# Last batch's attention output in tiles of 128 queries, transposed by DMA, in a fused attention and long-convolution kernel

## The chip, the cores and the metric

One core of one Trainium2 chip runs the whole kernel. Its engines run side by side, each through its own list of instructions in order, and wait for each other by semaphores: TensorE (PE: matmuls and transposes, into eight banks of PSUM), VectorE (DVE), ScalarE (ACT), GpSimd (POOL, here the queue that issues loads) and SyncE (SP, here the queue of stores and of DMA transposes). The metric is device time in microseconds (us) of one execution, the median of several runs.

## The reference, cut to what matters

Banded attention with eight global keys, and on its output a gated long convolution by FFT over the 768 positions. Shapes: batch 4, 8 heads, 768 positions, 64 per head (512 in all).

```python
# attention: keys 0..7 are seen by all, beyond them the last 96 positions
keep = (pos_k < 8) | ((rel >= 0) & (rel < 96))
scores = where(keep, q @ k.T / 8 - slope[h] * dist, -1e9)
a = softmax(scores); x = (a @ v)            # -> [B, 768, 512]
# gated long convolution
x1, x2, x3 = split(x @ w_proj, 3)
conv = irfft(rfft(x2, axis=1) * rfft(filter, axis=0), n=768)
out = (x1 * conv * x3) @ w_out              # [4, 768, 512] float32
```

## The kernel before

All four batches go through one pipeline; the work of batch b+1's attention is mixed with that of batch b's convolution.

**The order.** The program first collects operations in a `Plan` (each a small function with an engine or a choice of engines, the keys that it reads and writes, and the banks that it takes). `schedule` (L155) then replays a text, `ORDER` (L41): each word is an operation's number, an engine's letter (P, A, V, G for POOL, S for SP) and the PSUM banks; `i2b7` are two dummy matmuls into bank 7, which fill time at the start. So every engine's sequence, and the engine that does an operation that could go to ACT or DVE (`"AV"`), stands in this text.

**Attention.** Keys lie in seven tiles of 120 (the eight global keys stand beside each), `KL` = 120. For head pair `hp` and group `gi`, `scores` (L740) multiplies K by Q with the keys on the partitions: a tile of keys against the 216 queries that can see it (168 and 48 for the last two, `EW`). ACT takes the exponential (L773) into the tile `E`, DVE multiplies by a mask (L785, for two head pairs at once in batches 1 to 3). In `E` the queries of tile m start at column 248 m: 216 of data and a gap of 32 that is zero (set by `gaps`, L470 to L482; four operations, one for each head pair, each a memset of the gaps, L480, and one of ones at the end, L481).

`values` (L793) takes `E` as the stationary operand: 120 queries against the keys of their own tile (L808) and of the tile before (L813), 65 columns each, the 65th being the row sum. Queries come in the groups `GRP` = tiles (0,1), (2,3), (4,5,6); j is a half of the heads. Then a reciprocal on DVE (L837) and the scaling into `xn` on DVE (L832, one instruction) or ACT (L836, an instruction for every tile and head). `transpose_x` (L842) turns the tiles on PE (L854) into one bank and copies that (helper `copy`, L313) to `xT`, which has the 512 features on partitions and the 768 positions as columns. For batch 3 K and Q are not turned on PE but by 13 `dma_start_transpose` on SP's queue (`cross`, L395, L405).

**Convolution.** Gates x1, x3 are matmuls of `xT` with `w_proj` (`gate`, L922, L932), for a half s of the positions; x2 goes through a `butterfly` on DVE (L861 to L888) and a projection (`proj`, L993), then forward spectra (L1125), products with the filter's spectrum, inverse transforms (L1023, L1030), `mixed` (L1076, DVE, among it a doubling, L1092), `gated` (L1097, y = conv x gates), and the output matmuls (L1059). Their bank is scaled into an output tile `ot` of 128 positions by ACT (L317) or DVE (L319), and SP stores it (L1071). There are six buffers `ot`, taken in turn; the last tile of the last batch goes in two halves, in one buffer. `neg` is the negation of two inverse tables, which batch 3 uses.

Of the kernel before, what the change touches and what calls it, by code (L numbers as in the profile page):

```python
# [17 lines left out]
P = 128  # L18
# [10 lines left out]
def act(n):  # L29
    return 0.06 + n / 1200.0  # L30
# [11 lines left out]
0V 1V 2A 45S 3G 5V 4V 30V i2b7 17P0 18A 7G 47S 32G 49S 12P1 22P2 33A 56S 37V 34V 8V 19V 10V 20V 51G 21A 55G  # L42
46V 41V 53G 6V 40V 42V 23A 35G 24V 48V 13A 83P0 84A 25V i3b7 81P3 54G 14A 38A 36V 82V 52G 15V i2b7 149P23 85P1
27A 39V 44V 50V 115P45 57V 72G 58V 16A 26A 150A 60G 61G 93P0 87P6 86V 63G 89P7 88V 9V 95P1 80A 97P23 62G 31A
116A 43V 90V 91P6 92V 64G 98A 96V 74A 65G 151P45 152A 117P23 118A 99P67 101P45 119P23 94V 100A 102A 103P01 66G
11V 238G 155P45 67G 59S 120A 78A 28V 239G 211V 121P23 237G 29V 236G 104A 110P01 69G 235G 156A 212V 68G 105P67
213V 111V 122A 79A 234G 76A 153P45 128P23 106V 112V 123P01 107V 201P6 129V 233G 214V 232G 124V 108P7 130V 154A
215V 131P2 113P3 70G 125V 109A 244G 75A 157P45 114A 245G 126P7 132A 248G 127A 216V 158V 162P01 206A 246G 208A
133P7 73A 247G 135A 217V 240G 339P2 241G 243G 242G 137P3 159V 340A 220P7 229P45 163V 160P2 139A 164V 337P3
230A 202A 71G 252G 161V 251G 338V 226P01 221A 218P4 165P7 231V 145P3 203A 207A 219A 141P2 227A 166V 147A  # L50
371P45 184V 192V 134P3 254G 204A 335P0 193V 143A 457G 333P2 228A 249S 183V 195V 194V 209A 138P1 253G 334V 185V
336A 171P7 222P0 186V 140V 205A 136V 372A 223A 142P6 351P23 196V 369P01 173A 187V 144V 405P45 188V 197V 146P7
175P6 453G 198V 189V 352A 200V 345P2 148V 190V 347P3 370A 406A 177A 407P01 349P45 172P7 341P6 408A 350A 167P0
346V 77A 342A 168P1 452G 348V 250S 409V 169V 356P45 376P23 191V 256G 357A 451G 255G 174V 450G 343P0 344V 224P6
170V 377A 179P7 225A 455G 181A 374P45 354P23 456G 410P01 454G 353V 375A 199V 258P6 355A 259A 270P7 373V 359P45
378V 274P2 271A 411A 360V 412P67 413A 260P3 463G 284P0 361V 379P67 358V 414V 384P45 275A 469G 385V 380V 285A
282P2 261A 262P0 283A 364P23 386V 381V 460G 263A 470G 365V 278P4 264P5 552P6 466G 286V 279A 366V 462G 265A
467S 287V 459G 362P7 420P01 550P2 266P3 421V 464G 422V 363A 458G 415P45 553A 180P6 367P7 416V 556P0 267A 272P3
554P1 551A 368A 461G 268V 176P7 417V 557A 566P45 387P0 269V 273A 182V 276P3 555A 178V 418P1 388V 465G 382P2
568P67 567A 277A 588P45 419V 586P01 423P3 667G 474G 383V 389P2 569A 681G 587A 300P6 473G 471G 391A 280V 390P7  # L60
424V 393P2 296P3 671G 281V 672G 622P01 468S 589A 472G 624P45 673G 682G 570V 301A 394P6 392V 395A 292P7 302P2
297A 441V 625A 623A 442V 396V 558P3 293A 675G 562P4 563A 303A 294P5 290P0 425P1 291A 427A 288P6 295A 298P7
560P4 289A 443V 559V 689G 426P3 429P2 626V 444V 668G 576P01 561A 397P6 428V 431A 564P4 445V 299A 690G 577V
565A 687G 399A 475P2 446V 398P3 573P45 476A 593P67 578V 447V 574A 677G 304V 674G 688G 449V 571P01 448V 685G
401P2 400V 572A 430P4 594A 305V 479P5 432V 591P01 629P67 403A 306V 590V 627P23 480A 402P4 670S 487P5 680G 676G
592A 630A 579P0 477P1 575V 628A 488A 478A 307V 596P23 669S 595V 597V 483P5 404V 684S 581P67 580A 257G 308V
678G 489P1 437P4 582V 686G 598A 433P0 309V 490A 484A 679G 583V 601P23 435A 499P6 310V 584P5 602V 491P7 434P0
631V 500A 438P6 585V 603A 501P5 599P1 311V 637P23 436V 313V 439A 492A 502A 769S 481P7 600A 604P0 632P45 493P1
766S 768S 605A 773S 482A 312V 778S 618P0 638V 633V 494A 503V 639V 440V 634A 485V 611P7 614P1 504V 767S 610P2
771S 612A 495P6 318P3 770S 496A 606P2 486V 640P6 513P4 635P5 620A 619P0 319A 497V 616A 775S 776S 613V 514A  # L70
641A 636A 772S 315P1 608A 784P67 498V 781P45 621V 316A 658V 782A 779P23 785A 654P0 656A 615P1 509P4 507P5
505P6 607P7 314V 617V 517P0 780A 510A 659V 655P1 609V 661V 508A 657V 515P7 650P5 506A 516A 519P4 511P1 660V
518A 520V 662V 652A 663V 512A 774S 799P67 801P23 521V 800A 802A 642P5 664V 330P4 777S 841P67 683S 644A 786P23
522V 324P1 331A 665V 651P0 839P45 666V 842A 783V 325A 846P67 787A 703P1 840A 847A 704A 327P2 646P3 844P67 328A
806P45 523V 807A 653V 804P01 524V 695P2 691P4 693P5 317S 843V 805A 332S 525V 648A 789P01 788V 803V 808V 790V
705P3 845A 848V 692A 321P4 694A 696A 794P67 699P2 526V 795V 527V 791A 707P5 700A 796V 706A 849P01 322A 708A
530V 697P6 850V 814P23 647P7 698A 815V 809P45 851V 810V 531V 643P6 816A 854P01 544P2 645V 797P6 811A 792P3
649V 547P7 717P4 709P5 855V 798A 323S 329S 326S 793A 715P3 528V 711P6 856V 545A 710A 529V 817P2 852P0 712A
701V 812P5 716A 718A 541P1 857P3 320S 818A 532P4 713V 813A 719V 858A 542A 548A 720V 535P5 853A 825P3 714V 546S
834P2 533A 702V 879V 880V 829P0 725P4 727P1 882V 735P7 836A 726A 733P2 827A 881V 883V 721P6 538P4 536A 731P5  # L80
884V 210A 722A 732A 885V 835P3 729P6 539A 736A 728A 734A 870P5 730A 723P4 724A 888P7 887V 886V 830P2 738V
899P4 737V 739V 901P6 889A 910P7 900A 534S 543S 892P4 902A 740V 832A 905P6 837A 890P1 893A 741V 912P4 911A
913A 537S 819P3 549S 896P7 838V 865P4 891A 872A 897A 540S 894P1 903P5 895A 864P7 742V 821A 820P1 743V 904A
914V 907P5 867A 906A 908A 824P4 744V 898V 915V 831A 916P6 869P5 920P0 931P3 935P2 746V 909V 826A 745V 921A
937P4 917A 747V 932A 859P0 828V 933P3 922P6 938A 918P4 936A 833V 757P2 934A 940V 923A 751P6 860P3 939V 919A
925V 822A 748P1 754P4 924V 941V 752A 926V 942V 758A 760P2 755A 874P4 823V 943V 753S 927V 928V 944V 929V 862A
749A 945V 750S 756S 930V 948V 871A 763P3 759S 946V 876A 949V 947V 761A 762S 866A 875P1 961V 868V 877A 861A
764A 959V 863V 873V 950P2 951A 953P1 765S 954A 956P3 878V 952S 960V 975P2 955S 967P0 957A 962V 958S 976P 968P
971P3 963P1 972P 977A 969V 978S 970S 964P 973V 965A 974S 966S
# [108 lines left out]
class Fused:  # L198
# [16 lines left out]
    GRP = [(0, 1), (2, 3), (4, 5, 6)]  # L215
    Q0 = [0, 240, 480]
# [20 lines left out]
    def buffers(self):  # L237
# [48 lines left out]
        self.ot = [t(f"ot{i}", [P, DM], F32) for i in range(6)]  # L286
# [142 lines left out]
    def setup(self):  # L429
# [40 lines left out]
        for i in range(4):  # L470
            et = self.E[i]

            def gaps(e, et=et):
                if e == "A":
                    self.fill(et[:, :, 0:1488].rearrange("p h (m w) -> p h m w", m=6)[:, :, :, 216:248], 0.0)
                    self.fill(et[:, :, 1456:1536], 1.0)
                    return
                et = et.bitcast(F32)
                gap = et[:, :, 0:744].rearrange("p h (m w) -> p h m w", m=6)[:, :, :, 108:124]
                v.memset(gap, 0.0)  # L480
                v.memset(et[:, :, 728:768], ONES)  # L481
            g.op("AV", {"A": act(384) + act(160), "V": 0.38}, gaps, r=["idle"], w=[("E", i, c) for c in range(3)], name="gaps", bias=-3300)  # L482
# [59 lines left out]
    def inverse_tables(self):  # L542
# [31 lines left out]
        g.op("AV", {"A": 4 * act(P), "V": 4 * dve(P, 4)}, scaled, r=["part"], w=[("fwd", 3), "foldp"], name="foldp")  # L574
        g.op("AV", {"A": 2 * act(P), "V": dve(2 * P, 4)}, lambda e: [self.times(
            e, self.neg[:, n], self.inv[:, 2 - 2 * n], -1.0) for n in range(2)] if e == "A" else self.times(
            e, self.neg[:, ::-1], self.inv[:, 0:4:2], -1.0), r=[("inv", i) for i in range(7)], w=["neg"], name="neg")

    def distances(self):


# [279 lines left out]
    def butterfly(self, js):  # L861
# [4 lines left out]
        def op(cost, fn, r, w):  # L866
            g.op("V", cost, fn, r=[(k, j) for k in r for j in js], w=[(w, j) for j in js], name="bfly")
# [429 lines left out]
```

## Time and profile before

| | us |
|---|---|
| median of 3 runs | 166.29 (166.76, 165.31, 166.29) |
| the profiled execution | 164.31 |
| its span in the profile | 162.5 |
| PE busy | 154.4 (95%), 1608 matmuls |
| DVE busy | 151.9 (93%), 332 instructions |
| ACT busy | 149.8 (92%), 332 instructions |
| POOL busy | 77.2 (47%), 101 instructions |

The profiler records one execution: the span from the first to the last event, and in it the busy time of each engine. A row of the grouped views begins with the source line and the engine; L808 is line 808 of the kernel. Where a helper issues an instruction (L313 `copy`, L317 and L319 `times`, L328 `fill`), the tiles' names tell which step it is. In a row `out<-in 128x512 f16<-128x512 f32 x11 | 7.3, 675 | 0.0` stand the tiles, their partitions by elements, the count, the busy us, the mean ns and the idle time before them. The times of matmuls overlap, since PE works on several at once; how fast a stream of them goes is seen from their starts. A bracket in a row of the timeline is the engine's idle time just before it and what ended it; a link of the chain of waits has its start, its length and what it is.

### The profile page before, as it was taken

How to read it: one execution, taken by the hardware profiler on the slowest of the kernel's cores; microseconds unless marked ns; L12 is line 12 of the kernel's file. 1: busy time of each engine (PE TensorE's matmuls, PEld its weight loads, DVE VectorE, ACT ScalarE, POOL GpSimd, SP SyncE). 2: the span in 40 equal slices, each digit the busy share in tenths (PEclk: the TensorE clock that was granted, in tenths of full speed). 3: DMA queues.
4: the chain of work that ended last, by engine and by line, in shares of the span. 5: the costliest groups of instructions: out<-in, count | busy, mean ns of one | idle time of the engine just before them, and what ended most of it. 6: DMA issues, size and time to landing. Idle time of an engine off the chain costs nothing.

```text
span 162.5 us, 4271 instructions
## 1 busy us (share of the span) xinstructions
PE 154.4 (95%) x1608; PEld 93.4 (57%) x1608; DVE 151.9 (93%) x332; ACT 149.8 (92%) x332; POOL 77.2 (47%) x101
## 2 busy tenths in 40 slices
PE   7888989999999999999999999999999999999990
PEld 2444367565656866865657567455766664584450
DVE  5899979799999999999999999999999999999961
ACT  6979999999999999999899999999999998985961
POOL 7999198999999999999930000000000000000000
PEclk9999999999999999999999999999999999999999
DMA  5999999999999999999999984210083350001395
GB/s 164 215 148 164 167 158 171 171 166 160 184 155 149 125 139 131 143 145 139 149 150 165 141 161 93 67 44 0 11 205 115 130 196 0 4 0 61 142 363 210
DMA packets 85036, 21.95 MB, mean 135 GB/s; under 512 B 75664, under 2 KB 82072, under 8 KB 85016
## 3 DMA queue, kind: packets, MB, share of 16 engines
q0 software_dynamic: 73040, 12.11, 97.8%
q1 hardware_dynamic: 11976, 9.57, 23.0%
q8 instruction: 12, 0.20, 0.5%
q14 instruction: 8, 0.07, 0.1%
HBM read 25.40 MB, written 6.29 MB: 195 GB/s over the span
## 4 chain that ended last, share of the span: by engine, by line
PE 63%; ACT 17%; DVE 12%; issue 4%; POOL 1%; POOLq 0%
PE bank L932 18%; PE bank L1059 13%; PE bank L993 10%; ACT E L773 4%; PE bank L758 4%; PE bank L808 3%; PE bank L1125 3%; PE bank L813 3%; PE bank L854 2%; PE bank L1023 2%; PE bank L706 2%; ACT mask L626 2%; DVE E L785 2%; ACT h L317 1%; DVE g L946 1%
## 5 line engine op out<-in xcount | busy, mean ns | idle before, releaser
L932 PE MATMUL bank<-xT,w 128*128 128x384 f16 x256 | 49.5, 326 | 0.2
L773 ACT ACTIVATE E<-bank 128x864 f16<-128x864 f32 x48 | 41.4, 941 | 0.1
L932 PEld LDWEIGHTS <-w 128*128 128x128 f16 x256 | 23.3, 98 | 16.1 <-issue 1.7
L338 POOL DMA_DIRECT2D vn<-in_v_dram x28 | 27.8, 1019 | 0.4 <-DMA w<-in_moe_w_proj_dram 0.4
L338 POOL DMA_DIRECT2D kn<-in_k_dram x25 | 22.8, 930 | 3.3 <-DMA g<-in_moe_filter_fft_dram 3.3
L1059 PE MATMUL bank<-wo,y 128*128 128x512 f16 (+1 forms) x100 | 23.2, 371 | 0.0
L338 POOL DMA_DIRECT2D qn<-in_q_dram x25 | 22.4, 907 | 0.7 <-issue 0.6
L785 DVE TENSOR_TENSOR E<-E,mask 128x1728 f16<-128x1728 f16 x18 | 18.4, 1044 | 0.0
L317 ACT ACTIVATE ot<-bank 128x512 f32<-128x512 f32 (+1 forms) x23 | 14.3, 647 | 4.0 <-PE bank L1059 3.1
L317 ACT ACTIVATE x<-bank 128x384 f16<-128x384 f32 x31 | 17.0, 556 | 0.0
L993 PE MATMUL bank<-w,xs 128*128 128x512 f16 x64 | 16.5, 379 | 0.0
L313 ACT CAST ab<-bank 128x512 f16<-128x512 f32 x24 | 14.9, 648 | 1.3 <-PE bank L993 1.3
L808 PE MATMUL bank<-vn,E 128*128 128x65 f16 x224 | 15.4, 193 | 0.5 <-ACT E L773 0.5
L808 PEld LDWEIGHTS <-E 128*128 128x128 f16 x224 | 14.3, 97 | 2.5 <-issue 0.7
L313 ACT CAST eo<-bank 128x384 f16<-128x384 f32 x31 | 14.3, 555 | 1.0 <-PE bank L1030 1.0
L813 PE MATMUL bank<-vn,E 128*128 128x65 f16 x192 | 15.2, 193 | 0.0
L313 ACT CAST X<-bank 128x512 f16<-128x512 f32 x24 | 14.5, 635 | 0.1
L1059 PEld LDWEIGHTS <-y 128*128 128x128 f16 x100 | 9.2, 98 | 9.1 <-DVE y L1114 0.6
L758 PE MATMUL bank<-QT,KT 64*128 64x216 f16 (+2 forms) x224 | 14.1, 242 | 0.0
L832 DVE TENSOR_TENSOR xn<-bank,rc 128x512 f16<-128x512 f32 (+1 forms) x18 | 13.9, 779 | 0.1
L813 PEld LDWEIGHTS <-E 128*128 128x128 f16 x192 | 13.2, 97 | 0.8
L758 PEld LDWEIGHTS <-KT 64*128 64x128 f16 x224 | 7.9, 94 | 9.1 <-issue 7.6
(160 smaller groups left out, 337.1 us busy)
## 6 DMA issues: line engine op xcount, KB each, us to landing
out_dram<-ot SPq DMA_DIRECT2D x18, 256.0 KB
vn<-in_v_dram POOLq DMA_DIRECT2D x28, 120.0 KB, 5.9
kn<-in_k_dram POOLq DMA_DIRECT2D x16, 96.0 KB, 5.4
qn<-in_q_dram POOLq DMA_DIRECT2D x16, 96.0 KB, 5.1
out_dram<-ot SPq DMA_DIRECT2D x12, 128.0 KB
w<-in_moe_w_proj_dram POOLq DMA_DIRECT2D x4, 256.0 KB, 6.3
kn<-in_k_dram POOLq DMA_DIRECT2D x7, 120.0 KB, 5.4
g<-in_moe_filter_fft_dram POOLq DMA_DIRECT2D x1, 768.0 KB, 10.2
```

Of the source, the lines that this page charges most:

```text
L313: {"A": nc.scalar.copy, "V": nc.vector.tensor_copy, "G": nc.gpsimd.tensor_copy}[e](out, in_)
L317: self.nc.scalar.mul(out, in_, c)
L338: return self.g.op(eng, 0.57 + 0.00035 * nbytes[0] if eng == "G" else 0.5, lambda _: e.dma_start(dst, src), w=w, r=r, nbytes=nbytes, name= ...
L758: nc.tensor.matmul(bs[hh].f32()[:, off:off + w], self.KT[hs, hp, P * m:P * m + P], self.QT[hs, hp, KL * m:KL * m + w], start=(off == 0 and ...
L773: g.op("A", act(864), lambda _: nc.scalar.activation(eo, bs[0].two()[:, :, 0:432].rearrange("p h (m w) -> p h m w", m=2), Act.Exp, scale=s ...
L785: g.op("V", dve(1728, 2), lambda _: nc.vector.tensor_mul(ep, ep, mk), r=[("mask", h) for h in range(hs.start, hs.stop)], w=[("E", hp - 1, ...
L808: nc.tensor.matmul(o[:, n, hh], ef[:, at:at + P], vt[:, t, 2 * hp + hh, 0:D + 1], start=first, stop=(t == 0), skip_group_check=True)
L813: nc.tensor.matmul(o[:, n, hh], ef[:, at:at + P], vt[:, t - 1, 2 * hp + hh, 0:D + 1], start=False, stop=True, skip_group_check=True)
L832: nc.vector.tensor_mul(to, o[:, :, :, 0:D], rc.to_broadcast([P, 2, 2 * nt, D]))
L932: nc.tensor.matmul(bk.f32()[:, 0:h], self.w[:, c, o + P * j:o + P * j + P], self.xT[:, c, h * s:h * s + h], start=(c == 0), stop=(c == 3))
L993: nc.tensor.matmul(bk.f32(), src[:, c], w[:, c, DM:2 * DM], start=(c == 0), stop=(c == 3))
L1059: nc.tensor.matmul(bk.f32()[:, 0:n], y[:, c, P * t:P * t + P], self.wo[:, c, cs], start=(c == 0), stop=(c == 3))
```

## The change

Batch 3 only (`XCROSS`): its output goes in six tiles of 128 queries, not seven of 120, and to `xT` by DMA transposes.

- `E` has wide gaps of zeros: the starts are `EP`, 0, 336, 664, ... for all batches, so that 128 queries that start anywhere can be read from a key tile's columns, with zeros where that tile is not seen. `E` grows from 1536 to 1976 columns a head. `gaps` are eight operations, not four, with one memset for each gap. The 48 columns of the last key tile are copied behind the end (`e6`, two operations).
- `values_x` sums for each of the six tiles the key tiles that it can see, and scales into `xc`, [128 queries, 6 tiles, 512]; `xc` lies over `xn`.
- `cross_x` issues one `dma_start_transpose` for each tile (128x512, f16) on SP. The 28 PE transposes of batch 3 and its six copies to `xT` are gone. The second half's gates depend on the last group alone.
- Output buffers: three `ot` for batches 0 and 1; for batches 2 and 3 five that lie in `vn[0]`, the values of even batches, which nothing reads once batch 2's are summed. The halves of the last tile wait for the store that left their buffer.
- `neg` lies over a part of `fwd` and is computed once the filter's spectra are done. For batches 2 and 3 the butterfly's halving and the mix's doubling may go to ACT (`late`). `ORDER` is new throughout: engines, banks and places of all operations, POOL's loads among them.

```diff
-0V 1V 2A 45S 3G 5V 4V 30V i2b7 17P0 18A 7G 47S 32G 49S 12P1 22P2 33A 56S 37V 34V 8V 19V 10V 20V 51G 21A 55G
...
+0V 1V 2A 49S 4V 38V 3G 5V 51S 36G 6V 53S 34V i2b5 21P0 60S 57G 10V 8V 12V 22A 14A 26P1 7G 16P2 55G 27A 9V 50A
...
+    EP = [0, 336, 664, 984, 1296, 1600, 1768]
+    EL = 1928
+    XCROSS = (3,)
+    XGRP = [(0,), (1, 2), (3, 4, 5)]
...
-        self.EE = t("E", [P, 4, 2, 1536])
+        self.EE = t("E", [P, 4, 2, self.EL + 48])
...
-        self.xn = [t(f"xn{i}", [P, 2, 7, 2, D]) for i in range(2)]
+        xn = t("xn", [P, 4 * 7 * 2 * D])
+        self.xn = [xn[:, 28 * D * i:28 * D * i + 28 * D].rearrange("p (i t h d) -> p i t h d", i=2, t=7, h=2) for i in range(2)]
+        self.xc = xn[:, 0:6 * DM].rearrange("p (t c) -> p t c", t=6)
+        self.xturns = []
...
+        self.neg = self.fwd[:, 0:2]
...
-        self.neg = t("neg", [P, 2, P])
...
-        self.ot = [t(f"ot{i}", [P, DM], F32) for i in range(6)]
+        self.ot = [t(f"ot{i}", [P, DM], F32) for i in range(3)]
+        flat = self.vn[0].rearrange("p a b c -> p (a b c)").bitcast(F32)
+        self.ot += [flat[:, DM * i:DM * i + DM] for i in range(5)]
+        self.valued, self.sent = [], {}
...
-                gap = et[:, :, 0:744].rearrange("p h (m w) -> p h m w", m=6)[:, :, :, 108:124]
-                v.memset(gap, 0.0)
-                v.memset(et[:, :, 728:768], ONES)
...
+            for lo in (0, 3):
+                holes = [(self.EP[m] + 216, self.EP[m + 1] if m < 5 else self.EL, 0.0) for m in range(lo, lo + 3)]
+                if lo:
+                    holes[2:] = [(self.EL - 112, self.EL - 80, 1.0), (self.EL - 80, self.EL, 0.0)]
...
+                            nc.vector.memset(et.bitcast(F32)[:, :, x // 2:y // 2], ONES if c else 0.0)
...
+                if gi == 2 and self.b in self.XCROSS:
+                    last = self.EE[:, hp - 1:hp + 1].rearrange("p a h c -> p (a h) c")
+                    x, y = self.EP[6], self.EL
+                    g.op("AV", {"A": act(192), "V": 0.068 + 0.1}, lambda e: self.copy(
+                        e, last[:, :, y:y + 48], last[:, :, x:x + 48]), r=[("E", hp - 1, 2), ("E", hp, 2)],
+                        w=[("E", hp - 1, 3), ("E", hp, 3)], name="e6")
...
+    def values_x(self, j, c, slot):
...
+        parts = [[(m, (self.EP[m] if m < 6 else self.EL) + P * t - (KL * m)) for m in range(7)
+                  if KL * m < P * t + P and KL * m + self.EW[m] > P * t] for t in ts]
...
+                    for n, part in enumerate(parts):
+                        for m, at in part:
+                            nc.tensor.matmul(o[:, n, hh], ef[:, at:at + P], vt[:, m, 2 * hp + hh, 0:D + 1],
+                                             start=first, stop=True, skip_group_check=True)
...
+    def cross_x(self, c):
+        for t in self.XGRP[c]:
+            out = self.xT[:, :, P * t:P * t + P]
+            self.g.op("S", 1.3, lambda _, out=out, t=t: self.nc.sync.dma_start_transpose(out, self.xc[:, t]),
+                      r=[("xc", j, c) for j in range(2)], w=[("xT", j, c) for j in range(2)], nbytes=(128, 1024), name="xbar")
...
-        xs = [("xT", i, c) for i in range(2) for c in ((0, 1) if s == 0 else (1, 2))]
+        xs = [("xT", i, c) for i in range(2) for c in ((0, 1) if s == 0 else (2,) if b in self.XCROSS else (1, 2))]
...
-            o = self.outs % 6
+            o = self.outs % 3 if b < 2 else 3 + self.outs % 5
+            free = self.valued[:18] if b == 2 else []
+            held = [self.sent[o]] if last and t == 5 else []
```

More of the change, by code (lines that the diff above doesn't have):

```diff
@@ L47 @@
[L47 to L51, printed above, removed]
@@ L90 @@
+977V 969A 965A 970S 972P 966S 973A 978S 974S
 """
@@ L573, in scaled @@
                 self.times(e, f, f, self.part[:, s:s + 1])
[L574 to L577, printed above, removed]
+        g.op("AV", {"A": 4 * act(P) + 0.49, "V": 4 * dve(P, 4)}, scaled, r=["part"], w=[("fwd", 3), "foldp"], name="foldp")
     def distances(self):
@@ L667, in spectrum @@
                 e, h[:, o], pt(), sc), use=[b], w=[("h", s)], name="hs")
+        g.op("AV", {"A": 2 * act(P), "V": dve(2 * P, 4)}, lambda e: [self.times(
+            e, self.neg[:, n], self.inv[:, 2 - 2 * n], -1.0) for n in range(2)] if e == "A" else self.times(
+            e, self.neg[:, ::-1], self.inv[:, 0:4:2], -1.0), r=[("inv", i) for i in range(7)], w=["neg"], after=[x for x in g.ops if x.name == "fwd"], name="neg")
     def packed(self, s, src, keys, b):
@@ L854, in run @@
                     nc.tensor.transpose(tx[:, o:o + n], self.xn[j][0:n, i, t], self.ident[0:n, 0:n])
-        g.op("P", 2 * sum(0.0525 if t < 6 else 0.0558 for t in ts), run, acq=[b], r=[("xn", j, c), "ident"], name="trx")
+        self.xturns.append(g.op("P", 2 * sum(0.0525 if t < 6 else 0.0558 for t in ts), run, acq=[b],
+                                r=[("xn", j, c), "ident"], name="trx"))
         dst = self.xT[:, 2 * j:2 * j + 2, self.Q0[c]:self.Q0[c] + W]
@@ L859, in transpose_x, with butterfly @@
             w=[("xT", j, c)], name="xT")
-    def butterfly(self, js):
+    def butterfly(self, js, late=False):
         g, h, v, n = self.g, self.S // 2, self.nc.vector, len(js)
@@ L866, in op @@
         def op(cost, fn, r, w):
-            g.op("V", cost, fn, r=[(k, j) for k in r for j in js], w=[(w, j) for j in js], name="bfly")
+            g.op(cost if isinstance(cost, dict) else "V", cost, fn, r=[(k, j) for k in r for j in js], w=[(w, j) for j in js], name="bfly")
         g.op("V", dve(2 * h * n, 2), lambda _: v.tensor_add(ab[:, 0], xT[:, hs, 0:h], xT[:, hs, h:]),
@@ L924, in gate @@
         gt = self.gt[b % 2]
-        xs = [("xT", i, c) for i in range(2) for c in ((0, 1) if s == 0 else (1, 2))]
+        xs = [("xT", i, c) for i in range(2) for c in ((0, 1) if s == 0 else (2,) if b in self.XCROSS else (1, 2))]
         pts = []
@@ L977, in attention @@
         for js in ((0,), (1,)) if b == 0 else ((0, 1),):
-            self.butterfly(js)
+            self.butterfly(js, b > 1)
     def conv(self, b):
@@ L1068, in conv @@
                 g.op("AV", self.evac(n), lambda e, o=o, bk=bk, n=n, cs=cs: self.times(
-                    e, self.ot[o][:, cs], bk.f32()[:, 0:n], osc), use=[bk], after=done, w=[("ot", o, x) if m > 1 else ("ot", o)], name="ot")
+                    e, self.ot[o][:, cs], bk.f32()[:, 0:n], osc), use=[bk], after=done + free + held, w=[("ot", o, x) if m > 1 else ("ot", o)], name="ot")
                 rows = (slice(0, 64), slice(64, P)) if b == 0 and t < 5 else (slice(0, P),)
-                g.op("S", 0.5 * len(rows), lambda _, o=o, t=t, b=b, cs=cs, rows=rows: [nc.sync.dma_start(
+                self.sent[o] = g.op("S", 0.5 * len(rows), lambda _, o=o, t=t, b=b, cs=cs, rows=rows: [nc.sync.dma_start(
                     self.out[b, P * t + r.start:P * t + r.stop, cs], self.ot[o][r, cs]) for r in rows],
@@ L1074, in conv, with mixed @@
             g.bias = 0.0
-    def mixed(self, js):
+    def mixed(self, js, late=False):
         hs = slice(2 * js[0], 2 * js[-1] + 2)
@@ L1085, in op @@
         def op(fn, r, w, rate=2):
-            self.g.op("V", dve(512 * n, rate), fn, name="mix", r=[("eo", jp, jj, par) for jp in js
+            cost = {"V": dve(512 * n, rate), "A": act(512 * n)} if late and rate == 4 else dve(512 * n, rate)
+            self.g.op(cost if isinstance(cost, dict) else "V", cost, fn, name="mix", r=[("eo", jp, jj, par) for jp in js
                       for jj in range(2) for par in range(2)] + [(k, jp) for k in r for jp in js],
```

170 lines of the change are left out of this document (111 added, 59 removed).

## The prediction

> **What bounds the kernel now.** I read first the shares of the chain that ended last, then the span cut into five stretches, each with the busy time of every engine, then the chain itself, and the rows of the stretches that the change touches. The chain:
>
> ```profile
> PE 63%; ACT 17%; DVE 12%; issue 4%; POOL 1%; POOLq 0%
> ```
>
> TensorE (PE) carries most of it, but ACT and DVE have 29% together. The stretches say where. Columns: window, length, then busy time and instructions of PE, PE's weight loads, DVE, ACT and POOL, then the granted clock.
>
> ```profile
> 0.00:12.00 12.00, 9.69 (x74) 4.36 (x74) 9.75 (x44) 9.35 (x22) 10.84 (x25) 1.00 0.90 177
> 12.00:28.00 16.00, 14.33 (x235) 8.62 (x234) 14.56 (x40) 15.93 (x26) 12.17 (x15) 1.00 1.81 164
> ...
> 40.00:150.00 110.00, 109.84 (x1160) 69.18 (x1159) 109.11 (x205) 105.67 (x240) 42.20 (x48) 1.00 1.13 111
> 150.00:162.50 12.50, 8.81 (x47) 4.22 (x45) 7.57 (x23) 6.95 (x15) 0.00 (x0) 0.97 0.65 243
> ```
>
> Three regimes. From 12 to 28 us ACT is busy 15.93 of 16.00 and PE is not full: the start-up is ACT's, to the first gate matmul. From 40 to 150 us PE is busy 109.84 of 110, but DVE also 109.11 and ACT 105.67: PE is the bound, with less than a microsecond of room on DVE. From 150 us it is a tail. Three links of the chain show the three:
>
> ```profile
> 12.14 0.89 ACT E L773
> ...
> 122.52 0.75 PE bank L854 x14
> ...
> 158.85 0.60 ACT ot L317
> ```
>
> The first exponential starts at 12.14; the last batch's transposes of x stand on the chain for 0.75 us at 122.5; the last eviction starts at 158.85 and ends at 159.45, and the span ends at 162.5: 3.05 us are the last store.
>
> **PE's work.** A stream of 24 value matmuls, its first and its last row in the timeline:
>
> ```profile
> 115.39 0.19 PE L808 MATMUL bank<-vn,E 128*128 128x65 f16 x1
> ...
> 116.09 0.19 PE L813 MATMUL bank<-vn,E 128*128 128x65 f16 x1
> ```
>
> Starts lie 0.70/23 = 0.030 us apart. Two links of the chain, four matmuls of 512 columns and four of 384:
>
> ```profile
> 132.09 0.86 PE bank L993 x4
> 132.96 0.65 PE bank L932 x4
> ```
>
> They cost 0.215 and 0.163. The last batch has 104 value matmuls now (7 tiles x 8 heads, and 6 x 8 second halves); six tiles of 128 queries that sum 2, 3, 3, 3, 3 and 3 key tiles, 17 x 8 heads, make 136: +32 x 0.030 = **+0.96**. The 28 transposes that go cost 0.75/14 = 0.054 each by the chain's row: **-1.50**. PE: -0.54.
>
> **The last batch off PE.** Six copies of transposed x out of PSUM go, and the scaling of the values changes form. The tile of transposed x (count, then least, median and most ns, first and last start), a row of the timeline, and the groups of the scaling on DVE:
>
> ```profile
> L932 PE MATMUL bank<-xT,w x256: 322/326/337, 27.9 to 153.3; 128*128 128x384 f16 x128
> L313 ACT COPY xT<-bank x17: 550/607/815, 25.3 to 126.4; 128x480 f16<-128x480 f16 x13, 128x576 f16<-128x576 f16 x4
> L313 DVE COPY xT<-bank x7: 395/452/458, 31.4 to 85.1; 128x576 f16<-128x576 f16 x4, 128x480 f16<-128x480 f16 x3
> ```
> ```profile
> 113.30 1.81 ACT L836 ACTIVATE xn<-bank,rc 128x64 f16<-128x64 f32 x8
> ```
> ```profile
> L832 DVE TENSOR_TENSOR xn<-bank,rc 128x512 f16<-128x512 f32 x11 | 7.3, 675 | 0.0
> L832 DVE TENSOR_TENSOR xn<-bank,rc 128x768 f16<-128x768 f32 x7 | 6.6, 944 | 0.1
> ```
>
> The new order puts five copies fewer on ACT (5 x 0.607 = -3.0) and one fewer on DVE (-0.40), 12 pieces of 64 columns more on ACT (12 x 1.81/8 = +2.7), and on DVE two forms of 512 and two of 768 fewer (-3.24) against two of 256 and two of 384. A column costs (944-675)/256 = 1.05 ns, so a 256 is 0.41 and a 384 is 0.54, an estimate from these two rows: +1.9. DVE's balance is -1.34 - 0.40 = -1.74; ACT's is near nothing, with two copies of the last narrow key tile (128x192) added, at 0.3 to 0.4 each. As PE sets the end there, this counts nothing, unless DVE is what counts (a rival).
>
> **The wait that it adds.** The gates of the last batch used to wait for a PSUM copy. Now six crossbar transposes on SP's queue stand between: scaling, issue, transfer, landing. Nothing shows a 128x512 one; the nearest rows are the K and Q transposes of the same queue, and a store's issue on it:
>
> ```profile
> L405 SPq DMA_TRANSPOSE KT<-kn x7: 1205/1219/2362, 80.2 to 96.5; - x7
> L405 SPq DMA_TRANSPOSE QT<-qn x6: 1217/1306/2662, 77.7 to 97.8; - x6
> ```
> ```profile
> L1071 SPq DMA_DIRECT2D out_dram<-ot x30: 332/395/602, 99.9 to 159.5; - x30
> ```
>
> 1.22 us at the median, 2.66 at the worst. The first gates of the last batch need the first tile's transpose and the two of the second group. From the end of that group's value matmuls they need 1.81 (scaling on ACT) + 3 x (1.22 to 2.66) + 0.4 for the issue of a store that stands between them on SP + a landing, for which the nearest row is the tail's last store, 3.05: 8.9 to 13.2 us. In between the new order gives PE 20 matmuls of the projection, 6 of spectra and 12 of earlier outputs, 38 x 0.215 = 8.2 us, and the 72 value matmuls of the third group (2.2): 10.4. So from 1.5 us spare to 2.8 lacking. I take nothing, since the median lies near the low end; the cover is gone at (10.4 - 1.81 - 0.4 - 3.05)/3 = 1.7 us a transpose. The butterfly on DVE waits for the third group in the same way, with 1.0 more of scaling (12 pieces, not 8) and six gates (24 x 0.163 = 3.9, less the 2.2) more of cover. Queued behind these waits on SP are only stores of outputs, the next of them of a buffer that comes round five tiles later. By the Trainium skill, "DMA: Bandwidth & Descriptors", section "Anatomy of one DMA - SWDGE (gpsimd) path", a transfer that software starts has a fixed cost of some 2 us, most of it the confirmation of the last byte; by that the landing would be 1 us shorter than mine and the need 7.9 to 12.2. No row here shows a transpose's landing by itself, and the sum stays as it is.
>
> **The start-up.** The wide gaps are set to zero once, ahead of the first exponentials.
>
> ```profile
> L480 DVE MEMSET E<- x4: 218/218/218, 2.6 to 18.2; 128x192 f32 x4
> L481 DVE MEMSET E<- x4: 125/125/125, 2.9 to 18.5; 128x80 f32 x4
> ```
> ```profile
> L317 ACT ACTIVATE inr<-bank 128x256 f16<-128x256 f16 x1 | 0.4, 417 | 0.0
> L328 ACT ACTIVATE vn<-uw 128x256 f16<-128x256 f16 x1 | 0.4, 406 | 0.0
> ...
> L317 ACT ACTIVATE eo<-ident 128x128 bf16<-128x128 f16 x1 | 0.3, 292 | 0.0
> L328 ACT ACTIVATE vn<-uw 128x96 f16<-128x96 f16 x1 | 0.3, 272 | 0.0
> ...
> L626 ACT ACTIVATE mask<-eo 128x648 f16<-128x648 bf16 x6 | 4.5, 779 | 0.0
> ```
>
> DVE sets 4 x (0.218 + 0.125) = 1.37 us of them now, and 25 of together 2192 columns after: the two rows give (218 - 125)/112 = 0.83 ns a column and 59 a piece, so 3.3: +1.9, and ACT three fills more at 0.39 = +1.2. But the whole order of the start-up is new, so I sum ACT ahead of the first gates: fills +1.2; a cast and a Q copy of 768 columns, 0.86 each by 0.779 for 648, +1.7; five slope operations of 128x128, 5 x 0.292 = +1.46; four pieces of the inverse tables at 0.417, +1.7; eight scalings of 64 columns, +1.81; three masks fewer, -2.34; two copies of 512 fewer, -1.2; two fills of V fewer, -0.68: **+3.65** at most. ACT idles 12.00 - 9.35 = 2.65 in its first 12 us, and what fits in there is free: **+1.0** at least. Of this PE takes back what the order brings forward into the wait, six transposes (0.32) and four spectrum matmuls (0.87): -1.2. So the start-up costs -0.2 to +2.45, middle **+1.1**.
>
> **The edits with small or no price.** Two of the mix's doublings go from DVE to ACT, and loads change places on POOL (their issue in the second row):
>
> ```profile
> L1092 DVE TENSOR_SCALAR uw<-uw 128x1024 f16<-128x1024 f16 x3 | 1.8, 592 | 0.0
> ...
> L338 POOL DMA_DIRECT2D vn<-in_v_dram x28 | 27.8, 1019 | 0.4 <-DMA w<-in_moe_w_proj_dram 0.4
> ```
>
> -1.18 on DVE, at most as much twice over on ACT, and covered by PE's full stretch: nothing. One warm-up dummy less, the negation moved behind the spectra, and POOL's loads in a new order (two of Q and one of the weights come ahead of others of Q, K and V; POOL is busy 42 of 110 us in the middle): nothing, under the same cover; without it each moves the first gates by at most one load's issue, 1.02 us, and lies inside the start-up's bounds. Output buffers, three for the first two batches and five later: the trace shows evictions that wait for stores even with six.
>
> ```profile
> 157.55 0.69 DVE L319 TENSOR_SCALAR ot<-bank 128x512 f32<-128x512 f32 x1 [1.10 <-DMA out_dram<-ot]
> 157.64 0.38 ACT L317 ACTIVATE ot<-bank 128x256 f32<-128x256 f32 x1 [0.82 <-DMA out_dram<-ot]
> ```
>
> Both waits (1.10, 0.82) lie ahead of the last matmul's end and cost nothing. With three buffers such waits come in batches 0 and 1, where the stores have a batch's length; what is queued behind them on ACT are the exponentials. Taken: nothing; at worst 0.8 to 1.1 each. **The tail:** the last tile goes in halves, and the last eviction by the new order has 256 columns, 0.38 instead of 0.60: -0.22; the store behind it is half as large, which I take at nothing.
>
> **The sum.** -0.54 + 1.1 - 0.22 + 0 = +0.35 us. The profiled execution took 164.31 us, 162.50 of it the span and 1.81 around it; it would take 164.66. The median of the three runs before is 166.29, 1.98 above the profiled one, and I carry the difference over: **166.6**. Of the terms the start-up's is the weakest: with its bounds 165.3 to 167.9 (the other terms together give 0.1 more to each side).
>
> **The rivals.**
>
> *The crossbar is late (slower).* If a transpose costs its worst row, 2.66, the gates of the last batch wait: 2.8 us of PE idle. It decides from 1.7 us a transpose on. For it: half of the Q rows lie above 1.306, with a worst of twice that. Against it: those were issued beside POOL's loads, and the page's slices (4.06 us each) show POOL empty from the 24th on, 97 us.
>
> ```profile
> POOL 7999198999999999999930000000000000000000
> ```
>
> 166.6 + 2.8 = **169.4**.
>
> *The start-up costs in full (slower).* ACT and DVE are both full from 12 us on: if nothing of +2.45 is absorbed and DVE's 1.9 of memsets fall on the exponentials' path too, the whole of batch 0 moves by that. PE's full stretch then starts later, and nothing behind can give it back. 166.6 + (2.45 - 1.1) + 0.6 (a third of the memsets, those after 12 us) = **168.6**. For it: 15.93 of 16.00. Against it: in the first 12 us DVE too idles 2.25.
>
> *DVE is what counts (faster).* DVE is busy 109.11 of 110 in the middle; if PE's fullness is a matched pace (matmuls ordered to where their data come), what DVE loses counts: -1.74 - 1.18 = -2.92, with the start-up's middle (+1.1) and the tail (-0.22): -2.04, so **164.2**. For it: DVE's 12% of the chain. Against it: PE's 0.16 us of idle in 110. The Trainium skill, "Perfetto Trace Analysis", section "Identifying the Most-Contended Engine", holds that the busy time of matmuls is a bad measure, because they are pipelined, and so would not take 109.84 for a proof; the sum by this rule is this rival's.
>
> *The new buffers wait (the change gives back what it frees).* Two evictions of batches 0 or 1 wait for their stores, 0.9 each, with exponentials behind them: +1.8, **168.4**.
>
> **How the numbers follow.** Forecast 0.47 (166.6; its own range 165.2 to 168.0); late crossbar 0.15 (169.4); start-up in full 0.15 (168.6); DVE counts 0.20 (164.2); buffers 0.03 (168.4). 1% is 1.66 us, about what a measurement of this kernel tells from no change. Faster by more (below 164.6): most of the DVE case, 0.18, and 0.02 of the forecast's lower edge: 0.20. Slower by more (above 168.0): the late crossbar 0.15, most of the start-up case 0.12, the buffers 0.02 and 0.02 of the forecast's upper edge: 0.31. Within: 0.49. The range 164.0 to 169.2 leaves out half of the late crossbar (0.08) and half of the DVE case (0.10), so some 0.18.
>
> **What would show it.** In the changed profile: the first exponential later than 12.14 and the first gate matmul some 2 us later, with half of that taken back by 40 us (start-up); the stretch to the end of the values shorter; the SP rows of the six transposes near 1.2 us, and no idle time of PE in front of the last batch's gates (else the late crossbar); PE's busy share still above 99% in the middle, DVE's lower in the last 50 us (if PE's share falls there, DVE counts); no idle of ACT that ends on a store before 150 us (else the buffers). I am wrong if the start-up's shift isn't kept to the end, or if PE's full stretch gets shorter by more than 0.54 us.

## The result, and the profile after

| | before | after |
|---|---|---|
| median of the runs, us | 166.05 (4 runs, 165.31 to 166.76) | 176.81 (4 runs, 176.72 to 178.52) |
| the profiled execution / its span | 164.31 / 162.5 | 176.72 / 174.9 |

The change makes the kernel slower: ratio 1.0673, 95% interval 1.0592 to 1.0754. By the medians that is 10.8 us, far outside the range. Ratios and their intervals, here and below, leave out runs that lie more than 1.5% above the fastest of the same kernel; medians are of all runs.

The stretches of the changed kernel, columns as in the prediction (window, length, busy time of PE, weight loads, DVE, ACT, POOL, then the granted clock):

```profile
12.00:28.00 16.00, 12.60 (x179) 6.78 (x179) 12.45 (x41) 15.64 (x33) 12.16 (x15) 1.00 1.85 160
28.00:40.00 12.00, 12.00 (x150) 8.26 (x146) 11.77 (x29) 11.94 (x26) 11.20 (x15) 1.00 2.03 168
40.00:150.00 110.00, 101.39 (x1071) 63.19 (x1070) 97.57 (x186) 95.81 (x219) 42.51 (x49) 0.98 1.24 110
```

The loss is in the middle stretch, which was full: PE 109.84 before and 101.39 now, DVE 109.11 and 97.57, ACT 105.67 and 95.81. They idle 9 to 14 us each, so none of them is the bound: they wait for each other. The chain that ended last, its shares by engine, says the same. PE had 63% of it; now ACT and DVE have more than half together:

```profile
PE 35%; ACT 34%; DVE 23%; issue 6%; ACTq 0%; DVEq 0%
```

The longest waits between 40 and 150 us (engine, line it stood at, what it waited for, us in total, times, longest):

```profile
DVE E L798 <- ACT E L786: 10.9, 6, 3.4
...
ACT E L786 <- DVE E L798: 6.0, 5, 2.3
```

L786 is the exponential, L798 the mask (L773 and L785 before). A mask must wait for the exponentials that it multiplies. But an exponential that waits for a mask has no reason to: the columns of a group are written anew only when the values that read them are done, and those are PE's. Before, the 48 exponentials had next to no idle time in front of them; in the same group of the two pages:

```profile
L773 ACT ACTIVATE E<-bank 128x864 f16<-128x864 f32 x48 | 41.4, 941 | 0.1
```
```profile
L786 ACT ACTIVATE E<-bank 128x864 f16<-128x864 f32 x48 | 41.3, 898 | 8.2 <-DVE E L798 6.0
```

In the timeline of the changed kernel the two engines take turns, ACT first, then DVE:

```profile
42.78 0.89 ACT L786 ACTIVATE E<-bank 128x864 f16<-128x864 f32 x1 [1.19 <-DVE E L798]
```
```profile
41.63 1.06 DVE L798 TENSOR_TENSOR E<-E,mask 128x1728 f16<-128x1728 f16 x1 [0.75 <-ACT E L786]
...
45.12 1.06 DVE L798 TENSOR_TENSOR E<-E,mask 128x1728 f16<-128x1728 f16 x1 [1.22 <-ACT E L786]
```

The exponential at 42.78 starts when the mask of 41.63 is done. The waits in the built programs fit: 2 of the 48 exponentials wait for an earlier instruction of their own engine in the kernel before, 19 in the changed one. An exponential that waits for another exponential can only do so for the place that it writes. The two before wait for the exponential that wrote the very same columns. The 19 all wait for one of another pair of key tiles, which shares no column with them.

### The profile page after: what moved, and what is told of

The parts are those of the page before. It is cut to its first block, busy times and chain, and to the rows that moved or that the text cites. A ratio compares the mean times of both kernels' runs of the same rounds, so it can differ in the third digit from the quotient of the medians.

```text
span 174.9 us, 4354 instructions
## 1 busy us (share of the span) xinstructions
PE 157.0 (90%) x1611; PEld 94.7 (54%) x1611; DVE 151.7 (87%) x354; ACT 151.9 (87%) x338; POOL 76.7 (44%) x101
## 4 chain that ended last, share of the span: by engine, by line
PE 35%; ACT 34%; DVE 23%; issue 6%; ACTq 0%; DVEq 0%
ACT E L786 15%; PE bank L1146 9%; PE bank L1012 7%; PE bank L1078 7%; DVE E L798 6%; DVE g L1026 3%; ACT xT L323 3%; ACT xn L855 3%; PE bank L1108 3%; ACT x L327 3%; ACT mask L635 2%; DVE KT L323 2%; PE bank L878 2%; ACT X L323 2%; PE bank L1213 2%
## 5 line engine op out<-in xcount | busy, mean ns | idle before, releaser
L786 ACT ACTIVATE E<-bank 128x864 f16<-128x864 f32 x48 | 41.3, 898 | 8.2 <-DVE E L798 6.0
L798 DVE TENSOR_TENSOR E<-E,mask 128x1728 f16<-128x1728 f16 x18 | 18.8, 1045 | 10.9 <-ACT E L786 10.9
L348 POOL DMA_DIRECT2D vn<-in_v_dram x28 | 26.0, 959 | 1.3 <-DMA kn<-in_k_dram 1.3
L348 POOL DMA_DIRECT2D kn<-in_k_dram x25 | 21.4, 870 | 5.5 <-PE bank L719 5.0
L348 POOL DMA_DIRECT2D qn<-in_q_dram x25 | 21.6, 880 | 4.0 <-PE bank L771 3.8
L1078 PE MATMUL bank<-w,xs 128*128 128x512 f16 x64 | 15.8, 379 | 0.0
L327 ACT ACTIVATE x<-bank 128x384 f16<-128x384 f32 x30 | 14.9, 523 | 0.4 <-PE bank L1012 0.4
L827 PE MATMUL bank<-vn,E 128*128 128x65 f16 x168 | 12.0, 196 | 2.2 <-ACT E L786 2.1
L1026 DVE TENSOR_TENSOR g<-bank,x 128x384 f16<-128x384 f32 x24 | 12.9, 549 | 0.0
L827 PEld LDWEIGHTS <-E 128*128 128x128 f16 x168 | 10.9, 99 | 3.3 <-issue 2.2
L832 PE MATMUL bank<-vn,E 128*128 128x65 f16 x144 | 11.8, 196 | 0.0
L832 PEld LDWEIGHTS <-E 128*128 128x128 f16 x144 | 10.3, 99 | 1.0 <-issue 0.8
L851 DVE TENSOR_TENSOR xn<-bank,rc 128x512 f16<-128x512 f32 (+1 forms) x14 | 10.5, 772 | 0.0
```

What stands on the lines that cost most here:

```text
L327: self.nc.scalar.mul(out, in_, c)
L348: return self.g.op(eng, 0.57 + 0.00035 * nbytes[0] if eng == "G" else 0.5, lambda _: e.dma_start(dst, src), w=w, r=r, nbytes=nbytes, name= ...
L786: g.op("A", act(864), lambda _: nc.scalar.activation(eo, bs[0].two()[:, :, 0:432].rearrange("p h (m w) -> p h m w", m=2), Act.Exp, scale=s ...
L798: g.op("V", dve(1728, 2), lambda _: nc.vector.tensor_mul(ep, ep, mk), r=[("mask", h) for h in range(hs.start, hs.stop)], w=[("E", hp - 1, ...
L827: nc.tensor.matmul(o[:, n, hh], ef[:, at:at + P], vt[:, t, 2 * hp + hh, 0:D + 1], start=first, stop=(t == 0), skip_group_check=True)
L832: nc.tensor.matmul(o[:, n, hh], ef[:, at:at + P], vt[:, t - 1, 2 * hp + hh, 0:D + 1], start=False, stop=True, skip_group_check=True)
```

## The experiments

### Is it the steps in E?

Theory A: the program's layer that sets the semaphores compares the regions of `E` that instructions write. An exponential writes two key tiles of two heads, a region with a step from tile to tile. In the change the three pairs have the steps 336, 320 and 304, and regions with unequal steps are taken to overlap though no column is shared (false waits, from here on). Rival B: the new order puts the two too close, or another part of the change costs it.

```diff
 # e320: equal steps, same memory
-    EP = [0, 336, 664, 984, 1296, 1600, 1768]
+    EP = [0, 320, 640, 960, 1280, 1600, 1768]
 # egrp: equal steps inside each pair, gaps as wide as needed
-    VD = 96
+    VD = 92
-    EP = [0, 336, 664, 984, 1296, 1600, 1768]
-    EL = 1928
+    EP = [0, 336, 664, 1000, 1312, 1648, 1816]
+    EL = 1976
 # bgeo: the kernel before, its tiles 248 apart, shifted by a few columns
+    EP = [0, 252, 500, 750, 998, 1246, 1414]
-                        at = 248 * t if t < 6 else 248 * 5 + 168
+                        at = self.EP[t]
 ...
```

> The changed kernel with one size altered: key tiles 0 to 5 start every 320 columns in E instead of at 0, 336, 664, 984, 1296, 1600; memory, order and every instruction's size stay. Part of the computation that changes: the gaps ahead of key tiles 1 and 2 are 104 wide, not 120 and 112, so that some queries of batch 3 also sum columns of the tile before. Theory A: exponentials and masks that touch different columns of E wait for each other, because the pairs of tiles have unequal steps (336, 320, 304) and their strided regions are taken to overlap. Then, with equal steps, the 6.0 us in which ACT waits for a mask and most of the 10.9 us in which DVE waits for an exponential go, PE's idle time from 40 to 150 us falls from 8.6 us to under 2, and the time from 176.8 to 166 to 169. Rival B: the new order itself puts exponentials and masks too close, or the transposes by DMA and the longer start-up cost it: within 1.5 us of 176.8.

> As e320, but with gaps as wide as in the change, so that nothing of the computation changes: the step inside each pair of key tiles is 336, the pairs start at 0, 664, 1312 (E 48 columns longer), and the values' tiles have 92 columns a head instead of 96 to make room. Theory A: what counts is that the steps of the three pairs are equal, not that all tiles are equally spaced: within 1 us of e320, 166 to 169. Rival B: within 1.5 us of 176.8.

> The kernel before, with unequal steps inside the pairs of key tiles, 252, 250, 248 instead of 248 everywhere (starts 0, 252, 500, 750, 998, 1246); gaps are still zero where they are read; E is 8 columns longer and the gaps are set by 16 memsets instead of 8. Nothing else of the change is in it. Theory A: 2 to 4 columns bring the false waits into the kernel before: ACT waits for masks and DVE for exponentials for some us each, and the time rises from 166 by 5 to 12 us. Rival B: such small shifts cost only the memsets, some 0.5 us in the start-up: 166 to 167.

Measured: bgeo 173.1 us, ratio 1.0457 (1.0382 to 1.0531); e320 173.1, 1.0489 (1.0396 to 1.0582); egrp 173.1, 1.0459 (1.0379 to 1.054). bgeo settles the mechanism: with nothing of the change but steps of 252, 250 and 248 in place of 248, the same waits appear in the kernel before, and it loses 7.4 us:

```profile
ACT E L776 <- DVE E L788: 5.5, 4, 3.4
DVE E L788 <- ACT E L776: 5.0, 7, 1.4
```

In the built programs 22 exponentials of bgeo wait for their own engine, all for another pair of key tiles; in e320 and egrp 3 do, all for the same columns. egrp's pairs are not equally spaced (664, then 648), so it is the step inside an instruction's region that counts.

But the equal steps brought back only 3.7 us, where 8 to 11 had been expected: the time fits neither A nor B, and something else of the change costs too. The waits between exponentials and masks are gone in egrp; in their place stand these:

```profile
DVE g L1026 <- PE bank L1012: 9.4, 2, 8.8
PE bank L771 <- DMA QT<-qn: 8.4, 1, 8.4
ACT E L786 <- PE bank L771: 8.3, 1, 8.3
```

One wait, seen from three engines: PE stands 8.4 us at a score matmul of batch 3 for a tile of transposed Q. In e320 the chain shows that transpose, and what follows it:

```profile
90.19 9.03 DMA QT<-qn
99.21 0.14 issue
99.34 0.91 PE bank L771 x8
100.25 1.39 PE bank L1012 x4
```

Issued at 90.19, landed at 99.2. PE's own idle time in e320 is 5.7 us. And the four gate matmuls behind it take 1.39 us, where four took 0.65 (the prediction's row): the clock. In e320's stretches, the eighth number is the granted clock:

```profile
93.40:99.30 5.90, 0.20 (x2) 0.00 (x0) 2.17 (x4) 0.90 (x3) 0.00 (x0) 0.74 1.79 158
99.35:103.00 3.65, 3.65 (x16) 1.51 (x16) 1.32 (x4) 1.67 (x2) 0.00 (x0) 0.50 0.54 108
103.10:120.00 16.90, 16.90 (x208) 10.91 (x208) 15.82 (x28) 16.71 (x37) 0.00 (x0) 1.00 0.29 64
```

### Is it the sequence of the loads and transposes?

The new order loads tile 0 of Q eleventh of the thirteen tiles on POOL and transposes it eighth on SP, behind two copies for V; the scores need it first. egrp2 moves it forward; aord does the same in the changed kernel itself, with its unequal steps; egrp4 takes over the sequence of the kernel before whole.

```diff
 # words of ORDER, in the places that they had (S: transposes; q0 is 771S, its load 671G)
-776S 775S 770S 774S 772S 773S 782S 687S 688S 771S 777S 779S 778S 780S 781S
+772S 770S 775S 773S 771S 774S 776S 777S 782S 687S 688S 779S 778S 780S 781S
-678G 676G 680G 672G 677G 675G 679G 685G 684G 681G 671G 682G 683G
+676G 672G 678G 680G 677G 675G 671G 679G 681G 684G 685G 682G 683G
```

> egrp (equal steps in E), and the tiles of K and Q of batch 3 are loaded and transposed in the order of their need: tile 0 of Q is the fifth transpose on SP and its load the seventh on POOL, not the eighth (behind two copies for V) and the eleventh. Only places in the order change. Theory C: once the false waits are gone, the rest of egrp's loss is one wait, 8.4 us of PE for tile 0 of transposed Q at 93 us, and the 6.8 us at half clock behind it, which costs 3.4 us of matmul work. Then PE's longest wait after 40 us falls under 2 us, no stretch at half clock is left, and the time falls from 173.1 to 163 to 167. Rival D: the transposes as a whole are late (they land one after the other, 1.5 us apart, up to 100 us), so that another tile stalls PE in place of this one: 170 or more.

> The changed kernel with only the new places of K's and Q's loads and transposes, unequal steps in E kept. Theory C with A: the false waits hold PE back, so that it comes to batch 3's scores after the transposes anyway: no gain, 175 to 178. Rival D: the order of the transposes costs by itself: 173 or less.

> egrp with all of batch 3's loads (Q, K and V interleaved, q5 last) and transposes in the sequence that the kernel before has; places of PE, DVE and ACT as in the change. Theory C: the sequence of loads and transposes is what the change lost: the transposes land up to 99 us as before, PE waits less than 2 us at 93 us, 164 to 167. Rival D: the DMA engines, busy without a break up to 97 us, are the bound of this stretch whatever the sequence, and PE's order of the change comes to the scores 2.5 us earlier than the kernel before (93.3, not 95.8): PE waits 3 us or more at some tile, with a half-clock stretch behind, 168 to 172.

Measured: egrp2 170.4 us, ratio 1.0304 (1.023 to 1.0377); aord 176.9, 1.0725 (1.0678 to 1.0772); egrp4 170.9, 1.0342 (1.0272 to 1.0413). C fell, and D held, with egrp2 at the edge of its range: 2.7 us came back, and the wait moved on to a later tile of Q, in egrp2's timeline (the traced execution took 172.2 us):

```profile
97.17 0.27 PE L771 MATMUL bank<-QT,KT 64*128 64x216 f16 x2 [0.86 <-DVE X L1241]
102.27 0.72 PE L771 MATMUL bank<-QT,KT 64*128 64x216 f16 x6 [4.83 <-DMA QT<-qn]
```

With the sequence of the kernel before, PE still waits 3.5 us (egrp4's waits have one of 3.5, again for Q). So the sequence is only a part: egrp4 is 2.2 us below egrp by the medians, and the intervals overlap. In egrp4 PE comes to these scores at 93.5 us, where the kernel before came at 95.8; and the tile that it waits for lands at 97.0, where it landed at 94.7. The transposes as a whole are late for a PE that comes early; what in the new order brings PE there earlier, no run separates. aord, as expected with A, confirms that none of this shows while the false waits are there: a PE that is late anyway does not wait for Q.

### Is it V's loads beside the transposes?

By the semaphore events in the traces, transposes land 1.2 to 3.6 us apart in e320 while loads are in flight (the first seven, from 83.3 to 95.6 us), and some 0.5 us apart after V's last load has landed at 99.4. egrp5 therefore holds back six of V's seven loads until the last tile of Q is transposed; egrp6 only until the eighth transpose, with V's tiles in the order of their need. Both also move the two copies for V on SP behind all the transposes, and no run tells this from holding back the loads. after6 is egrp6 with the change's own steps.

```diff
 # load_rows, batch 3 (egrp6; egrp5 has t == 6 and column 767)
+        if b == 3 and t == 1:
+            go = o.fn
+            o.fn = lambda e: [self.nc.gpsimd.tensor_copy(self.warm[0:1, 0:1], self.QT[0:1, 0, 511:512]), go(e)]
 # ORDER: V's loads stand behind the transposes
-694G 689G 692G 691G 690G 693G ... 781S
+781S 689G 690G 691G 692G 693G 694G
```

> egrp2 (equal steps, Q and K in the order of need), and six of the seven loads of V of batch 3 wait until the last tile of Q is transposed (one small copy on POOL reads it ahead of them); the copies of V's global rows come last on SP. Theory E: the transposes land 1.3 to 1.5 us apart because they share the DMA engines with V's loads (0.5 us apart in the kernel before, once the loads are over), so that without these all land by 95 us, PE waits less than 1.5 us at the scores, no half-clock stretch is left, and the time falls to 161 to 165. Rival F: the loads of Q and K land too late by themselves, or V then comes too late for its first use at 113 us: 168 or more.

> egrp5 with the six loads of V held back less long (until tile 3 of Q is transposed, the eighth of thirteen) and in the order of their need. In egrp5 the wait for transposed Q was gone, but the values' matmuls of batch 3 waited 2.8 us for V at 104 us, with 3.4 us at half clock behind, in some of its runs (median 165.3, its undisturbed runs 163.7). Theory E: with V some 4.5 us earlier, nothing of PE's waits is left after 40 us but what the kernel before has; the time is then that of the change's own terms: start-up +0.5 (PE has done 24.8 us of work by 40 us, 25.3 in the kernel before), PE's work -0.5, tail -0.2, so 164.5 to 165.5, or down to 162 if PE has fewer small waits. Rival G: some other wait shows up behind these (the transposes of x, stores), 166.5 or more.

> The changed kernel with egrp6's sequence of loads and transposes and V's loads held back, but with its own unequal steps in E: egrp6 and this differ in the steps alone (and in the values' tiles of 92 or 96 columns a head). Theory A: the false waits between exponentials and masks cost by themselves what they cost in bgeo, some 7 us or more: 170 to 175, and the gain of the held-back loads is small, since PE comes late to batch 3's scores anyway. Rival H: the 3.7 us that the equal steps brought in egrp are all that the false waits cost, and the loads are the larger part: 166.5 to 168.5.

Measured: egrp5 165.3 us, ratio 0.995 (0.9908 to 0.9993); egrp6 163.73, 0.9925 (0.9897 to 0.9953); after6 176.2, 1.0638 (1.057 to 1.0706). E held in its main point: in egrp5 no transpose makes PE wait. The last one has landed at 98.1 us, where it was 101.6 in e320, though not by 95. The median, 165.3, lies between E's range and F's, and what F feared shows in the traced execution, which is one of the three longest of ten (168.3 us): V is late at its first use:

```profile
POOL warm L360 <- DMA QT<-qn: 19.5, 1, 19.5
...
PE bank L882 <- DMA vn<-in_v_dram: 2.8, 1, 2.8
```

In egrp6 that is gone too. Its full stretch is as full as that of the kernel before, and PE has the chain again:

```profile
40.00:150.00 110.00, 109.96 (x1169) 69.03 (x1167) 109.34 (x209) 105.27 (x243) 42.60 (x50) 1.00 1.26 114
```
```profile
PE 85%; ACT 10%; DVE 1%; issue 1%; DVEq 0%
```

So egrp6 beats both kernels: 13.1 us below the change and, by under 1%, 1.4 us below the kernel before that ran beside it.

after6 is the pair to read beside egrp6: 176.2 against 163.7, and the steps in `E` (with 92 or 96 columns of a head of V) are all that differs. Its longest waits are those of the changed kernel again: masks for exponentials 10.7 us, exponentials for masks 6.0. The false waits alone cost 12.5 us by the medians (11.8 by the two ratios), as much as the whole loss or a little more. Rival H, that the loads were the larger part, fell; A's 170 to 175 was too low. The two delays overlap rather than add up: removing the loads' delay first gains 0.6 us (176.8 to 176.2, within the noise), removing the false waits first 3.7 (to 173.1), both 13.1.

## Why the prediction was wrong, point by point

**The step that failed** is the wide gaps. I costed them as memsets alone ("The wide gaps are set to zero once") and gave the exponentials and masks no term at all, because their sizes are unchanged. Their regions changed: from one step of 248 to three. That made waits where nothing is shared, 12.5 us by after6 and egrp6. The full stretch, which was not to get shorter by more than 0.54 us, lost 8.5 us of PE's busy time. Of all my rivals none was about `E`. The change part by part asked what each instruction costs, not whether its place in memory still tells it apart from its neighbours.

**POOL's loads** were put at nothing, "covered by PE's full stretch", at most 1.02 us if uncovered. The cover was the wrong one: the DMA engines are busy for nine tenths or more of nearly every slice of the page up to 97 us, in both kernels, so a load that is put ahead of another delays it. Once the false waits are gone, the late transposes cost 9.4 us by the medians (egrp against egrp6); egrp's profiled run shows a wait of 8.4 and 3 us of work at half clock behind it, which cost 1.5. That is not the price of the new sequence alone: with the old one, egrp4 still lost 5.4 us, for there PE comes to the scores earlier and the tile lands later than before. In the changed kernel as it stands all this is hidden behind the false waits.

**The start-up** is later by its first gate, and by its work about as forecast. The first gate matmul starts at 30.9, not 27.9, a microsecond more than I had put:

```profile
L1012 PE MATMUL bank<-xT,w x256: 322/326/525, 30.9 to 164.6; 128*128 128x384 f16 x128
...
L918 SPq DMA_TRANSPOSE xT<-xn x6: 1188/1206/1676, 125.6 to 133.4; - x6
```

The columns of all matmuls that PE has started by 40 us come to 29.7 us of work against 30.9 (at 2.4 columns per ns: the prediction's row has four of 512 in 0.86 us). That is 0.9 to 1.2 us behind, by how matmuls that overlap are counted, where I had +1.1. Some of it is false waits: in egrp, without them, it is 0.4 to 0.7. The memsets came out as worked: 25 of them, 3.3 us in all.

**The late crossbar** did not come: the six transposes of x take 1.19 to 1.68 us each (the second row above; 1.19 to 1.86 in egrp6, and decisive would have been 1.7 for all), and no engine waits for them, in the changed kernel or in egrp6. The landing, taken as 3.05, comes 1.1 to 2.9 us after the issue by the semaphore events of the two traces. One reading in that rival is off: POOL's row is empty from the 22nd slice on, 85 us; it is the DMA engines that are full up to 97. The new forms on DVE were right: 0.42 and 0.55 us for 256 and 384 columns, estimated at 0.41 and 0.54. The two copies of the narrow key tile took 0.45 each, not 0.3 to 0.4.

**The tail** was mis-sized. The last eviction is 0.38 us, as forecast, and ends at 171.49, but the span ends at 174.9: 3.4 us for the last store, not 3.05. SP issues three stores in a row there:

```profile
170.68 0.42 DVE L329 TENSOR_SCALAR vn<-bank 128x256 f32<-128x256 f32 x1 [1.10 <-PE bank L1146]
170.75 0.27 PE L1146 MATMUL bank<-wo,y 128*128 128x256 f16 x1
170.91 1.34 SPq L1158 DMA_DIRECT2D out_dram<-vn  x3
171.11 0.38 ACT L327 ACTIVATE vn<-bank 128x256 f32<-128x256 f32 x1 [0.22 <-ACT vn L327]
```

The store that I took at nothing queues behind two others, and the -0.22 became about +0.1.

**The sum without the waits.** egrp6 shows what is left when both are gone: -1.4 us, by its interval -1.7 to -0.8, where I had +0.35. PE's work (-0.54), the start-up by its work in egrp (+0.4 to +0.7) and the tail (+0.1) make 0 to +0.3, so 1.4 to 1.7 us of gain isn't in my terms. Where it comes from isn't shown. The rival that DVE counts put the sum at -2.04, near to what came, and no run tested it. The profiled execution of egrp6 took 165.28 us, with a stretch of 3.4 us at half clock in the start-up that its other runs can't have had in full (they took 163.7 to 164.4, with a mean clock of 0.996 or more, where it has 0.99), so its trace can't be set against that of the kernel before for a microsecond.

## What to carry to other kernels

When a layout changes, look at the waits of the built program before the durations: two instructions that write different columns of one tile may still be made to wait for each other, and a step that is equal in all of them avoids it (a tile of its own for each might too; that was not tried). When one wait is removed and little comes back, look for the next that stood behind it: delays that overlap don't add up (here 12.5 and 9.4 us each alone, 13.1 together), and the second shows its price only when the first is gone. A queue of loads that keeps the DMA engines full is a bound of its own, and what is put into it early delays what is needed first.

## What the runs showed of the hardware

**Idle PE can cost twice.** Behind a long wait of PE the granted clock falls to half. In the changed kernel PE is idle for 2.8 us at 81 us, and 3.41 us at half clock follow:

```profile
80.90:83.70 2.80, 0.25 (x5) 0.13 (x3) 2.40 (x3) 0.52 (x2) 2.80 (x5) 1.00 2.57 142
83.70:87.10 3.40, 3.16 (x30) 2.48 (x30) 3.25 (x6) 2.29 (x5) 3.40 (x4) 0.50 1.88 128
87.20:100.00 12.80, 12.80 (x173) 8.86 (x171) 12.24 (x26) 12.35 (x39) 0.91 (x1) 1.00 1.72 145
```

Behind 3.46 us of idle time (egrp4) half clock lasts 3.41 us as well. Behind 4.83, 5.7 and 8.4 us (egrp2, e320, egrp) it lasts 6.83 us, part of it over while PE still waits. Shorter idle stretches do it in some traces only. Those of 2.7 to 2.8 us did in the changed kernel, aord, bgeo and egrp5, but not in after6 (2.78 us at 81.5). A stretch of 1.66 us in after6 and one of 1.43 in egrp6 were followed by 3.41 us at half clock; others of that length weren't. The Trainium skill, "TensorE: Matmul & The Clock Gate", section "What's actually happening", states a free-running window of 3.413 us and half rate after at least one idle window. The lengths agree; an idle stretch of 2.8 us, shorter than the window it names, was enough in four of five traces here.

**DMA transposes beside loads.** In e320 a tile of 128x512 takes SP 1.2 to 2.3 us to issue. With several queued and no load in flight, each lands some 0.5 us behind the one before it; with loads in flight they land 1.2 to 3.6 us apart. The Trainium skill, "Advanced Engine Details and Errata", section "X-Bar Transpose (TRN2)", calls them as fast as regular DMAs and expects 350 to 400 GB/s. Here 131 KB in 0.5 us, an estimate of 260 GB/s, is below that, and holds only when they run alone.
